# Lightning attention and a leaky-ReLU MLP on one core: the down projection in pairs of groups, partly with seven block products for eight

## The chip, the cores and the metric

The kernel runs on one core of one Trainium2 chip. The metric is device time in microseconds of one execution. TensorE (PE) multiplies; VectorE (DVE), ScalarE (ACT) and GpSimd (POOL) do the elementwise work; SyncE (SP) issues nearly all DMAs, which run on 16 DMA engines.

## What is computed

Inputs are q, k, v of 4 batches, 8 heads, 768 tokens and 64 channels, one decay per head, and two weight matrices. Attention is linear with a decayed state, in blocks of 64 tokens; its result, 3072 tokens by 512, goes through an MLP:

```
x = attn.transpose(0, 2, 1, 3).reshape(3072, 512)
h = x @ w_in                      # 512 -> 2048
g = np.maximum(0.01 * h, h)
out = g @ w_out                   # 2048 -> 512
```

The weights come as float64.

## The kernel before, in words

Tokens are handled in 24 chunks of 128, four chunks to a group (512 tokens), six groups g. The 2048 hidden features are eight slabs p of 256, each of two halves f of 128. Every operand of a large product is split into three parts, a head h, a low part l and a third one m made from both, and each product is three matmuls, h with h, l with l and m with m.

There are two stages. In the *up stage* (with attention interleaved, seen as lines L313, L403 and the att tiles) `up(g, p)` multiplies a slab of w_in with a group: 24 matmuls of 512 columns into one of three rotating banks b (L640), ScalarE scales the bank between the parts (L658) and writes the leaky ReLU into one of two buffers gs (L661), and one DMA stores it to a DRAM tile G (L664). In the same stretch w_out is turned from float64 to float32 (`w_out`, L569 to L585, L617) and then split (`w_out_parts`, L621, L591 to L602) over the w_in slab that is no longer needed.

In the *down stage* each unit, one (g, p), is loaded from G (L675) and split by ScalarE (L682) and VectorE (L683, L685) into one of four ring slots, which lie over the X operands of the up stage. `down(g, p)` has the activations as the stationary operand and w_out as the moving one, so the result lies with tokens in partitions (L700):

```
nc.tensor.matmul(acc[tb][z // 2][:, cols], lhsT=ring[j][z][:, f * T + tb * P:f * T + (tb + 1) * P],
                 rhs=W[pp][z][:, f * d_model:(f + 1) * d_model][:, cols],
```

Four token blocks use the eight banks (psc, po, b and pt). At a group's end ScalarE copies one bank of a token block (L722), VectorE adds the other (L729), and one store of 256 KB in rows of 2 KB goes to the output (L732).

The order on every engine is fixed when the program is built. `Plan.add` takes each operation with an engine, an estimated time, the keys that it reads and writes, and a rank; `Plan.emit` runs through them by earliest start and rank, with one serial DMA queue and lags between engines (3.5 us after a DMA, plus a slack that `move` may set), and emits them in that order. At run time every engine takes its instructions in this order, SP its DMAs too, and each waits for the real events. The list `seq` gives the ranks: rounds of attention, ups, weight steps, then the loads ("dl") and products ("dn") of the down stage.

## Time and profile before

| | us |
|---|---|
| median of 3 runs (lowest, highest) | 611.26 (610.93, 611.92) |
| span of the profiled execution | 609.2 |
| what the median has around that span | 2.1 |
| TensorE busy | 597.9 |
| VectorE busy | 314.0 |
| ScalarE busy | 269.0 |
| up stage, first full TensorE stretch to the first down product | about 47 to 343 |
| down stage | about 343 to 609 |

The profiled execution has its own time only as the span, from its first to its last instruction; the runs' times include what lies around it. A group row of the profile gives line, engine, operation and tiles, then total busy time and the mean of one in ns, then idle time of the engine just before and who ended it. A timeline row gives start and length in us. Matmuls overlap, so their pace is read from a run of them and not from the mean of one.

### The profile page before, as it was taken

The numbers are of one execution on the slowest core, as the hardware profiler recorded it, in microseconds if no ns is written. First come the engines' busy times: TensorE is split into PE (matmuls) and PEld (weight loads), VectorE is DVE, ScalarE is ACT, GpSimd is POOL, SyncE is SP. The second block draws the span as 40 slices with busy tenths as digits, with TensorE's granted clock in tenths as the row PEclk, the third lists the DMA queues.
The fourth block names the chain that finished last, engine by engine and source line by source line (L and its number), as shares of the span: only waits on it lengthen the run. The fifth ranks groups of instructions, "written<-read, shape, count | busy, mean of one in ns | idle before, by whom it ended". The sixth has DMA issues, their size and how long they took to land.

```text
span 609.2 us, 12932 instructions
## 1 busy us (share of the span) xinstructions
PE 597.9 (98%) x5386; PEld 495.6 (81%) x5386; DVE 314.0 (52%) x418; ACT 269.0 (44%) x430; POOL 86.8 (14%) x90
## 2 busy tenths in 40 slices
PE   7899999999999999999999999999999999999997
PEld 6687888888888878888788888888888888888886
DVE  5999764334243426326366745545454544635531
ACT  4688974444455646555577522222222313214111
POOL 1654412104133004104000000000000000000000
PEclk9999999999999999999999999999999999999999
DMA  9998774667888878886686843524333343333201
GB/s 213 232 272 245 221 203 124 173 133 199 199 213 238 212 227 214 216 244 210 233 300 217 290 145 103 173 69 139 138 104 131 112 138 105 138 104 122 86 1 69
DMA packets 147754, 105.18 MB, mean 173 GB/s; under 512 B 123632, under 2 KB 124400, under 8 KB 147696
## 3 DMA queue, kind: packets, MB, share of 16 engines
q1 hardware_dynamic: 147552, 104.36, 58.9%
q8 instruction: 42, 0.69, 0.5%
q14 instruction: 16, 0.13, 0.1%
q10 hardware_dynamic: 144, 0.00, 0.0%
HBM read 68.69 MB, written 35.65 MB: 171 GB/s over the span
## 4 chain that ended last, share of the span: by engine, by line
PE 92%; DVE 4%; DMA 2%; ACT 1%; issue 0%; POOL 0%; SPq 0%; DVEq 0%; ACTq 0%
PE b L640 40%; PE b L700 18%; PE po L700 11%; PE psc L700 11%; PE po L313 4%; PE pt L700 4%; PE psc L313 4%; DMA g<-gs 1%; DMA att<-in_v_dram 1%; DVE w L584 1%; DVE w L585 1%; DVE wm L602 1%; PE pt L403 1%; DMA att<-in_k_dram 1%; DVE wl L596 0%; DVE wh L593 0%
## 5 line engine op out<-in xcount | busy, mean ns | idle before, releaser
L682 ACT ACTIVATE xh<-att 128x1024 fp32r<-128x1024 f32 x48 | 50.7, 1060 | 148.7 <-PE b L700 140.7
L683 DVE SCALAR_TENSOR_TENSOR xl<-att,xh 128x1024 fp32r<-128x1024 f32 x48 | 58.6, 1223 | 98.6 <-ACT xh L682 98.6
L640 PE MATMUL b<-xm,wm 128*128 128x512 f32 (+2 forms) x392 | 104.5, 393 | 0.5 <-ACT b L658 0.5
L640 PE MATMUL b<-xl,wl 128*128 128x512 f32 (+2 forms) x392 | 103.4, 388 | 0.6 <-DVE wl L596 0.6
L640 PE MATMUL b<-xh,wh 128*128 128x512 f32 (+2 forms) x392 | 103.2, 387 | 0.8 <-ACT xh L507 0.8
L640 PEld LDWEIGHTS b<-xh,wh 128*128 128x128 f32 x392 | 73.0, 188 | 15.9 <-ACT xh L507 0.9
L640 PEld LDWEIGHTS b<-xl,wl 128*128 128x128 f32 x392 | 72.8, 188 | 15.6 <-DVE wl L596 1.0
L640 PEld LDWEIGHTS b<-xm,wm 128*128 128x128 f32 x392 | 71.5, 188 | 15.7 <-ACT b L658 0.9
L658 ACT ACTIVATE b<-b 128x512 f32<-128x512 f32 (+2 forms) x97 | 56.1, 580 | 60.3 <-PE b L640 60.1
L661 ACT ACTIVATE gs<-b 128x512 f32<-128x512 f32 (+2 forms) x97 | 56.8, 591 | 44.9 <-PE b L640 38.8
L700 PE MATMUL b<-wl,xl 128*128 128x512 f32 x192 | 74.8, 390 | 0.0
L700 PE MATMUL b<-wh,xh 128*128 128x512 f32 x192 | 74.8, 390 | 0.0
L685 DVE SCALAR_TENSOR_TENSOR xm<-xl,xh 128x1024 fp32r<-128x1024 f32 x48 | 58.7, 1226 | 4.7
L462 POOL TENSOR_TENSOR att<-att 128x256 f32<-128x256 f32 x40 | 35.0, 876 | 57.2 <-DVE att L459 55.9
L700 PEld LDWEIGHTS b<-wl,xl 128*128 128x128 f32 x192 | 36.1, 188 | 7.4
L700 PEld LDWEIGHTS b<-wh,xh 128*128 128x128 f32 x192 | 36.0, 188 | 7.5
L423 POOL TENSOR_TENSOR att<-att 128x512 f32<-128x512 f32 (+1 forms) x20 | 24.2, 1211 | 96.2 <-DVE att L383 47.4
L452 DVE TENSOR_TENSOR att<-psc,att 128x512 f32<-128x512 f32 x24 | 16.5, 690 | 41.0 <-PE psc L313 41.0
L584 DVE TENSOR_SCALAR w<-w 128x512 int32<-128x512 int32 x32 | 19.2, 599 | 35.4 <-ACT w L578 35.3
L700 PE MATMUL po<-wm,xm 128*128 128x512 f32 x96 | 37.4, 390 | 0.0
L700 PE MATMUL po<-wh,xh 128*128 128x512 f32 x96 | 37.4, 390 | 0.0
L700 PE MATMUL po<-wl,xl 128*128 128x512 f32 x96 | 37.4, 390 | 0.0
(73 smaller groups left out, 805.4 us busy)
## 6 DMA issues: line engine op xcount, KB each, us to landing
att<-g SPq DMA_DIRECT2D x48, 512.0 KB, 3.3
g<-gs SPq DMA_DIRECT2D x47, 512.0 KB, 4.0
raw<-in_moe_w_in_dram SPq DMA_DIRECT2D x16, 512.0 KB, 5.4
raw<-in_moe_w_out_dram SPq DMA_DIRECT2D x16, 512.0 KB, 4.7
att<-in_k_dram SPq DMA_DIRECT2D x48, 128.0 KB, 4.2
att<-in_v_dram SPq DMA_DIRECT2D x24, 256.0 KB, 4.4
out_dram<-gs SPq DMA_DIRECT2D x23, 256.0 KB, 2.1
wo<-w SPq DMA_DIRECT2D x8, 512.0 KB, 5.9
```

Of the source, the lines that this page charges most:

```text
L313: nc.tensor.matmul(dst[HALF[cols]], lhsT=lhsT[HALF[rows]], rhs=rhs[HALF[rows]], start=start, stop=True, skip_group_check=True)
L423: add(eng, us, lambda: e.tensor_tensor(o, x, _bc(pow_q, 2, 2)[:, :, m, :], op=ALU.mult), ["fq", dep], [f"qsT{i}"])
L452: add("DVE", 0.69, lambda: nc.vector.tensor_tensor(sc, psc[:, :, lower, :], decay, op=ALU.mult), ["psc", "fk"], ["sc"])
L462: add("POOL", 0.7, lambda new=new, j=j: nc.gpsimd.tensor_tensor(state[(j + 1) % 4], new, _bc(lam_c, 2, D), op=ALU.mult), [f"st{j % 4}", "f ...
L584: add("DVE", 0.42, lambda: nc.vector.tensor_scalar(d, d, 3, None, op0=ALU.logical_shift_left), [], [key])
L640: nc.tensor.matmul(dst, lhsT=w[z][:, kk * 2 * P + f * P:kk * 2 * P + (f + 1) * P], rhs=x[z][:, kk, toks], start=start and kk == 0, stop=kk ...
L658: add("ACT", ns, lambda b=b: nc.scalar.activation(out=b, in_=b, func=AF.Copy, bias=0.0, scale=S + 1.0), [], [kb], rank=-1.5)
L661: add("ACT", ns, lambda b=b, r=r: nc.scalar.activation(out=r, in_=b, func=AF.Prelu, bias=0.0, scale=1.0 / WS, alpha=0.01), [kb], [f"gs{jg} ...
L682: add("ACT", 1.05, lambda: nc.scalar.activation(out=h, in_=graw[j], func=AF.Copy, bias=0.0, scale=NEAR), reads, wr("h"))
L683: add("DVE", 1.25, lambda: nc.vector.scalar_tensor_tensor(l, graw[j], 1.0, h.bitcast(F32), op0=ALU.mult, op1=ALU.subtract), reads + [f"rh{ ...
L685: add("DVE", 1.25, lambda: nc.vector.scalar_tensor_tensor(m, l.bitcast(F32), -S, h.bitcast(F32), op0=ALU.mult, op1=ALU.add), [f"rh{j}", f" ...
L700: nc.tensor.matmul(acc[tb][z // 2][:, cols], lhsT=ring[j][z][:, f * T + tb * P:f * T + (tb + 1) * P], rhs=W[pp][z][:, f * d_model:(f + 1) ...
```

## The change

Groups are handled in three pairs. The operands of the down product change places: w_out is stationary in pieces of 128x128, the activations move 512 tokens at a time, and the result lies with output features in partitions. All three parts of a product now accumulate in one bank, with the scale moved into the up stage's ReLU.

In pair 0, and for slabs p of 4 and more in the other pairs, products are plain: 24 matmuls for a slab and a group (`plain`). For p below 4 in pairs 1 and 2 the products of a slab are taken as 2x2 blocks (two halves f, two halves of the output features, two halves of the tokens of both groups), and seven block products stand for eight (`strassen`), 12 matmuls to a unit of two slabs. Four bank sets X, Y, Z, V take the products; `copy_banks` copies one set to another with ScalarE, `add_banks` adds one set to another through the two halves of gs buffer 0 with ScalarE and VectorE.

The seven products need sums of operands. Those of the activations are made by VectorE in the up stage (`sums`, four operations of 128x256 for each of 16 ups, three of them stored by DMAs of their own, next to the four blocks themselves in one DMA), into a DRAM tile BB of a pair; the other stores to G are split in two by token half. Those of w_out are made in pair 0 (`w_sums`), from the float32 copy in DRAM, over w_out's own second quarter and over memory of attention. The third part of w_out is made in two steps, VectorE and ScalarE (`minus`). The ring has five slots, and a unit is loaded straight into the slot's third part (`unit`). The order of ups in groups 2 to 4 alternates slabs above and below 4, and the slack given to loads of w_out is 0.75 in place of 4.0.

A finished bank leaves by a 32x32 block transpose of VectorE from PSUM into one of two halves of gs buffer 0, and eight stores of 32 partitions each, in pieces of 128 bytes (`leave`).

```diff
     SUBL, FIRST = 0.75, -8.0
 
+    NS = 4
+    LEAD = 8.0
+    WSLACK = 0.75
     DV = 10
...
+    HT = T // 2
+    KINDS_B = ("1", "7", "2", "3", "5", "6", "4")
+    BB = [[dram.tile([P, 7 * 2 * T], F32, name=f"b{r}_{u}", tag=f"b{r}_{u}") for u in range(NS // 2 if r else 0)] for r in range(NG // 2)]
+    G = [{p: dram.tile([P, 4 * T], F32, name=f"g{r}_{p}", tag=f"g{r}_{p}") for p in range(NS if r else 0, NP)} for r in range(NG // 2)]
...
-        move(1.6, get, after, [f"raw{j}"])
+        move(1.6, get, after, [f"raw{j}"], slack=WSLACK)
...
+    def minus(us, x, key):
+        add("DVE", us, lambda: nc.vector.tensor_tensor(x(2), x(1).bitcast(F32), x(0).bitcast(F32), op=ALU.subtract),
+            [key.format("h"), key.format("l")], [key.format("m")])
+        add("ACT", 0.85 * us, lambda: nc.scalar.activation(out=x(2), in_=x(2).bitcast(F32), func=AF.Copy, bias=0.0, scale=1.0 / (S + 1.0)),
+            [], [key.format("m")])
...
+    def w_sums(p):
+
+        j, jr, main, rest = SK[0], SK[1], staging[0], staging[1]
+        b = [main[:, i * NQ:(i + 1) * NQ] for i in range(4)] + [rest[:, i * NQ:(i + 1) * NQ] for i in range(3)]
...
+        def sub(o, x, y, op, reads, k_):
+            add("DVE", 0.42, lambda: nc.vector.tensor_tensor(b[o], b[x], b[y], op=op), reads, k_)
+
+        sub(5, 0, 1, ALU.subtract, j, jr)
+        sub(1, 1, 3, ALU.add, [], j)
+        sub(4, 1, 0, ALU.subtract, j, jr)
+        sub(6, 2, 4, ALU.subtract, j, jr)
+        for key, us, x, src, k_ in ((f"w{{}}{p}", 0.42, lambda z: W[p][z][:, NQ:2 * NQ], b[1], j),
+                                   (f"e{{}}{p}", 0.95, lambda z: more(z, p), rest[:, :3 * NQ], jr)):
+            h, l, m = [key.format(z) for z in "hlm"]
+            add("ACT", 0.9 * us, lambda x=x, src=src: nc.scalar.activation(out=x(0), in_=src, func=AF.Copy, bias=0.0, scale=NEAR / S), k_, [h])
+            add("DVE", us, lambda x=x, src=src: nc.vector.scalar_tensor_tensor(x(1), x(0).bitcast(F32), -S, src, op0=ALU.mult, op1=ALU.add),
+                k_ + [h], [l])
+            if p == NS - 1 and k_ is jr:
+                add("ACT", 0.0, free_lows, [], jr + [m])
+            minus(us, x, key)
...
-        move(1.5 * (hi - lo) / GC + 0.1,
-            lambda: nc.sync.dma_start(out=G[g][p].rearrange("p (f t) -> p f t", f=2)[:, :, toks], in_=y), [f"gs{jg}"], [f"G{g}{p}"], slack=GSLACK)
...
+        if p >= NS or g < 2:
+            d = G[g // 2][p].rearrange("p (f h g t) -> p f h g t", f=2, h=2, g=2)
+            for i in range(2):
+                a, e = max(lo * C, i * HT), min(hi * C, (i + 1) * HT)
+                if a < e:
+                    move(0.75 * (e - a) / HT + 0.1, lambda i=i, a=a, e=e: nc.sync.dma_start(
+                            out=d[:, :, i, g % 2, a - i * HT:e - i * HT], in_=y[:, :, a - lo * C:e - lo * C]),
+                        [f"gs{jg}"], [f"G{g}{p}{i}{lo}"], issue=0.3, slack=GSLACK)
+            return
+        sums(g, p, y.rearrange("p f (h t) -> p f h t", h=2), f"gs{jg}")
...
+    def sums(g, p, y, kg):
+
+        z = spare(g, p)
+        (z0, k0), (z1, k1), (z2, k2) = z
+        (b11, b12), (b21, b22) = [[y[:, f, i, :] for i in range(2)] for f in range(2)]
+
+        def op(o, x, x2, a, reads, writes):
+            add("DVE", 0.42, lambda: nc.vector.tensor_tensor(o, x, x2, op=a), reads, writes, rank=-1.0)
+
+        d = BB[g // 2][p // 2].rearrange("p (k c g t) -> p k c g t", k=7, c=2, g=2)[:, :, p % 2, g % 2, :]
+
+        def store(k, o, key, name):
+            move(0.5, lambda: nc.sync.dma_start(out=d[:, k], in_=o), [key], [f"{name}{g}{p}"], issue=0.15, slack=GSLACK)
+
+        op(z0, b12, b11, ALU.subtract, [kg], [k0])
+        op(b12, b22, b12, ALU.subtract, [], [kg])
+        store(4, z0, k0, "T4")
+        op(z1, b12, b11, ALU.add, [kg], [k1])
+        move(1.6, lambda: nc.sync.dma_start(out=d[:, :4], in_=y.rearrange("p f h t -> p (f h) t")), [kg], [f"B{g}{p}"], slack=GSLACK)
+        store(5, z1, k1, "T5")
+        op(z2, b21, z1, ALU.subtract, [kg, k1], [k2])
+        store(6, z2, k2, "T6")
...
+    acc = {"X": flat[:2], "Z": flat[2:], "Y": [b1[0], b2], "V": [b1[1], bank["pt"]]}
+    ACC = {"X": ["X0", "X1"], "Z": ["Z0", "Z1"], "Y": ["b10", "b2"], "V": ["b11", "pt"]}
...
+    KINDS = {1: (0, "X"), 5: (1, "V"), 6: (-1, "Z"), 2: (2, "X"), 7: (-2, "Z"), 3: (-3, "Y"), 4: (3, "Z")}
+    BANKS = [[("X", 0), ("X", 1), ("Z", 0), ("Z", 1)], [("Y", 0), ("Y", 1), ("V", 0), ("V", 1)]]
...
+        add("DMA", 1.5, go, keys, wr("m"))
+        add("ACT", 1.05, head, [f"rm{j}"], wr("h"))
+        add("DVE", 1.25, low, [f"rm{j}", f"rh{j}"], wr("l"))
+        add("DVE", 1.25, middle, [f"rh{j}", f"rl{j}"], [f"rm{j}"])
+        return j
+
+    def product(dst, j, col, lhs, first=False, n=T):
+        for z in range(3):
+            nc.tensor.matmul(dst, lhsT=lhs(z), rhs=ring[j][z][:, col:col + n], start=first and z == 0, stop=z == 2,
+                             skip_group_check=True)
+
+    def strassen(pr, t, u, lead):
+
+        g = 2 * pr
+        ps_ = (2 * u, 2 * u + 1)
...
+        w, d = KINDS[t]
+
+        def go():
+            for i, p in enumerate(ps_):
+                for c in range(2):
+                    product(acc[d][c], j, i * T, lambda z, p=p, c=c: operand(z, p, w)[:, c * P:(c + 1) * P],
+                            first=t in (1, 5) and u == 0 and i == 0)
+        add("PE", 0.227 * 12, go, [f"r{z}{j}" for z in "hlm"] + [f"{'w' if w >= 0 else 'e'}{z}{p}" for z in "hlm" for p in ps_],
+            ACC[d])
...
+    def plain(pr, p, gi, lead, last=False, banks=None):
...
+        def go(fs, cs, lo=0, n=T):
+            for f in fs:
+                for c in cs:
+                    d, i = BANKS[gi][c]
+                    product(acc[d][i][:, lo:lo + n], j, f * T + lo,
+                            lambda z, f=f, c=c: W[p][z][:, f * 2 * NQ + c * P:f * 2 * NQ + (c + 1) * P], first=pr == p == f == 0, n=n)
+
+        if not last:
+            add("PE", 0.227 * 24, lambda: go((0, 1), range(4)), reads, [ACC[d][i] for d, i in BANKS[gi]])
+            return
+        for c in banks:
+            d, i = BANKS[gi][c]
+            very_last = pr == NG // 2 - 1 and gi == 1 and c == banks[-1]
+            for half in range(2 if very_last else 1):
+                k = ACC[d][i] + (f"half{half}" if very_last else "")
+                n = T // (2 if very_last else 1)
+                add("PE", 0.227 * 6 * (0.53 if very_last else 1.0), lambda c=c, half=half, n=n: go((0, 1), (c,), half * n, n),
+                    reads + ([ACC[d][i]] if very_last else []), [k])
+                leave(pr, gi, c, acc[d][i], ACC[d][i], k, half * n, n)
+
+    def leave(pr, gi, c, b, kb, k, lo, n):
+        nonlocal n_o
+        o, n_o = n_o % 2, n_o + 1
+        y = gs[0][:, o, lo:lo + n]
+        add("DVE", 0.1 + 0.6 * n / T, lambda: nc.vector.transpose(out=y, in_=b[:, lo:lo + n]), [kb, k], [f"o{o}"] + (["gs0"] if n_o <= 2 else []), rank=-1.5)
+
+        def store():
+            for a in range(4):
+                for m in range(lo // HT, (lo + n) // HT):
+                    t0 = (2 * pr + m) * T + gi * HT
+                    nc.sync.dma_start(out=out[t0:t0 + HT, c * P + a * C4:c * P + (a + 1) * C4].rearrange("(b i) j -> i b j", i=C4),
+                                      in_=y[a * C4:(a + 1) * C4, m * HT - lo:(m + 1) * HT - lo].rearrange("i (b j) -> i b j", j=C4))
+
+        add("DMA", 1.7 * n / T, store, [f"o{o}"], [], rank=-1.5)
+
+    def copy_banks(d, s):
+        for i in range(2):
+            add("ACT", 0.6, lambda i=i: nc.scalar.copy(acc[d][i], acc[s][i]), [ACC[s][i]], [ACC[d][i]], rank=-1.5)
+
+    def add_banks(d, s):
+        for i in range(2):
+            y, key = gs[0][:, i, :], [f"o{i}"] + (["gs0"] if n_o == 0 else [])
+            add("ACT", 0.6, lambda i=i, y=y: nc.scalar.copy(y, acc[s][i]), [ACC[s][i]], key, rank=-1.5)
+            add("DVE", 0.72, lambda i=i, y=y: nc.vector.tensor_tensor(acc[d][i], acc[d][i], y, op=ALU.add), [f"o{i}"], [ACC[d][i]], rank=-1.5)
...
+    ORDER = [4, 0, 5, 1, 6, 2, 7, 3]
+    steps = [(g, p) for g in range(2, NG) for p in (ORDER if g < NG - 1 else range(NP))]
...
-    for g in range(NG):
-        for p in range(0, NP, 2):
-            seq += [("dl", g, p), ("dl", g, p + 1), ("dn", g, p)]
+            if p == NS - 1:
+                seq.append(("fr",))
+    for pr in range(NG // 2):
+        def s(t, u):
+            return "s", pr, t, u
+
+        def n(p, gi, r=pr):
+            return ("n", r, p, gi) if p < NP - 1 else ("l", r, p, gi, (0, 1, 2, 3) if gi == 0 else (2, 3, 0, 1))
+
+        late = [n(p, 1, pr - 1) for p in range(NS, NP)] if pr else []
+        if pr:
+            seq += [late[0], s(1, 0), late[1], s(1, 1), ("copy", "Z", "X"), late[2], s(6, 0), late[3], s(6, 1), ("copy", "Y", "Z"),
+                    s(5, 0), s(5, 1), ("add", "Y", "V"), s(7, 0), s(7, 1), ("add", "V", "Z"),
+                    s(3, 0), n(4, 0), s(2, 0), n(5, 0), s(3, 1), s(2, 1), n(6, 0), s(4, 0), s(4, 1), n(7, 0)]
+        else:
+            i = seq.index(("up", NG - 1, NP - 1))
+            seq[i:i] = [n(0, 0)]
+            seq += [n(0, 1), n(1, 0), n(1, 1), ("ws", 0), n(2, 0), n(2, 1), ("ws", 1), n(3, 0), n(3, 1), ("ws", 2), n(4, 0), n(5, 0), ("ws", 3), n(6, 0), n(7, 0)]
+    seq += [n(p, 1) for p in range(NS, NP)]
```

## The prediction

> **What bounds the kernel now.** I read the page's busy shares first, then the chain that ended last, then windows, and then the groups, DMA issues and timeline of the places that the change touches.
>
> ```profile
> span 609.2 us, 12932 instructions
> PE 597.9 (98%) x5386; PEld 495.6 (81%) x5386; DVE 314.0 (52%) x418; ACT 269.0 (44%) x430; POOL 86.8 (14%) x90
> PE 92%; DVE 4%; DMA 2%; ACT 1%; issue 0%; POOL 0%; SPq 0%; DVEq 0%; ACTq 0%
> ```
>
> TensorE is busy for 98% of the span and carries 92% of the chain; the rest of the chain lies in the first 47 us, which the change hardly touches. So a matmul taken out is worth its full pace, as long as nothing else then comes late. The windows show how much room the others have:
>
> ```profile
> 180.00:345.00 165.00, 164.24 (x1679) 135.58 (x1678) 77.76 (x118) 98.58 (x169) 25.52 (x28) 1.00 0.80 236
> 215.00:260.00 45.00, 44.52 (x536) 36.53 (x535) 18.12 (x32) 25.61 (x46) 10.30 (x12) 1.00 0.84 225
> 300.00:345.00 45.00, 45.00 (x201) 37.25 (x200) 27.96 (x29) 30.75 (x49) 0.00 (x0) 1.00 0.78 268
> 432.00:605.00 173.00, 173.00 (x767) 143.42 (x766) 81.45 (x76) 39.30 (x46) 0.00 (x0) 1.00 0.30 103
> ```
>
> After the length come PE, PEld, DVE, ACT and POOL, the granted clock, the DMA share and GB/s. In the up stage (180 to 345) the DMA engines are 80% busy and VectorE 47%. In the down stage (432 to 605) TensorE has no idle time, the clock is 1.00, VectorE is at 47% and the DMA engines at 30%. The stage's grain, from the chain in order of time, the groups, the DMA issues and the timeline:
>
> ```profile
> 368.93 2.72 PE po L700 x12
> L683 DVE SCALAR_TENSOR_TENSOR xl<-att,xh 128x1024 fp32r<-128x1024 f32 x48 | 58.6, 1223 | 98.6 <-ACT xh L682 98.6
> L459 DVE TENSOR_TENSOR att<-att,psc 128x256 f32<-128x256 f32 x40 | 16.4, 410 | 1.1 <-POOL att L462 1.0
> L383 DVE STREAM_TRANSPOSE att<-raw 128x512 f32<-128x512 f32 x2 | 1.3, 688 | 0.0
> g<-gs SPq DMA_DIRECT2D x47, 512.0 KB, 4.0
> 95.73 3.80 SPq L374 DMA_DIRECT2D raw<-in_k_dram  x7
> 604.50 1.11 PE L700 MATMUL pt<-wm,xm 128*128 128x256 f32 x8
> 605.71 0.76 DVE L729 SCALAR_TENSOR_TENSOR gs<-pt,raw 128x256 f32<-128x256 f32 x2 [1.72 <-PE pt L700]
> L732 SPq DMA_DIRECT2D out_dram<-gs x25: 332/338/383, 382.1 to 606.6; - x25
> ```
>
> Twelve matmuls take 2.72 us, 0.2267 each. The last matmul ends at 605.6, the last store's issue starts at 606.6 and the span ends at 609.2: a tail of 3.6 us, 2.6 of them after that issue. Each of the 25 output stores costs SP 0.34 us.
>
> **The change part by part.** *Matmuls.* Pairs 1 and 2 replace, for p below 4, 192 matmuls by 7 x 2 x 12 = 168 of the same shape: 48 fewer in all, -10.9 us, all on the path. The last bank, in halves, takes 12 x 0.139 = 1.66 in place of 1.36, where before 8 halves took 1.11 in place of 0.91: +0.1.
>
> *Unit preparation.* There are 60 units in place of 48, each with one load, one ACT copy (1.06) and two VectorE operations (1.22): 12 x 2.45 = +29 us of VectorE. A seven-product unit feeds 2.72 us of TensorE and needs 2.45 us of VectorE, so in a row of six of them VectorE stands at 90%. The cover is the ring of five units. Over a pair VectorE has 22 x 2.45 + 8 transposes and 4 bank adds of 0.69 = 62 us against 81.6 of TensorE. I cost this at nothing by itself; it makes every late unit slow to catch up.
>
> *Weight sums* (four in pair 0): 1.7 us of small subtractions and 2.7 of splitting on VectorE, 2.4 on ACT each. With 16 units VectorE has 57 of pair 0's 87 us; hidden by that. The two-step third part adds 8 x 1.06 of ACT in the last group of the up stage, 30.75 + 8.5 of 45 us there; hidden. Zero-cost markers moved from VectorE to POOL issue nothing.
>
> *Sums of activations* (16 ups): 64 operations of 128x256 at 0.41 (the L459 row) are 26 us of VectorE, in 165 us with 87 idle. Three stores of 128 KB more for each, 6.3 MB; at the window's 225 GB/s for a share of 0.84 that is 24 us of DMA, share 0.80 to about 0.94. In most of the other 33 ups one store becomes two, +0.35 us of SP each. The buffer gs is the narrow place: an up is 24 x 0.2267 = 5.44 us, so from the last ScalarE write of one up to the first write two ups later there are about 7.5 us. Before, a landing of 4.0 fits. Now two VectorE operations (0.82) and one more issue (0.4) come ahead of the large store, and the DMA engines are fuller: 5.3 us without queueing. The large store's wait stands in SP's queue ahead of later k, q and v loads; a late landing holds ScalarE's Prelu and with it the scaling of the next bank, which TensorE waits for. In before ScalarE waited twice on such a landing (2.4 us in the waits), and TensorE's idle time in 215 to 260 is 0.5 us. Weight loads are now planned with 0.75 us of slack where they land in 4.7, which can hold ScalarE likewise. Ends: 0 (all fits) and +8 (half a microsecond in each of the 16). More than the 0.8 us of idle TensorE in 180 to 345 can't be gained. I take +2, four such events of the size seen.
>
> *Output, the main term.* A 512-token bank now leaves as transposed 32x32 blocks: the transpose costs 0.69 like the operation that it replaces, but one store of 0.34 becomes eight on the same SP queue, of 32 KB each in 128-byte pieces. No such store is in the trace. The nearest row is the transposed load of the same 32 KB: seven in 3.80 us, 0.54 with the slow second one of a run, 0.5 otherwise. The far row is the plain store, 0.34 + 0.05 between issues. I take 0.5, since the shape is the same and only the direction differs: 4.0 to 4.4 us of SP for each leave, 16.8 for four in a row, where banks are ready every 1.36 us.
>
> The tail, from the end of the first of the last four banks: first leave transposed by 0.75, its stores issued 0.8 to 5.1; second 5.1 to 9.1; third 9.1 to 13.1; first half 13.1 to 15.1; the second half shares its buffer with the third leave and waits for that to land (12.6 + 2.0) and for its transpose: stores 15.1 to 17.1, the last starting at 16.6. The end is 2.6 later, 19.2. TensorE ends at 2.72 + 1.66 = 4.4. Tail 14.8 in place of 3.6: +11.2. With 0.39 an issue it is 11.7: +8.1.
>
> The same queue inside: when a pair's second group leaves at the start of the next pair, TensorE goes on with six seven-product units. Counted again from the first bank's end: the copies of Z to Y need the fourth leave's transpose (10.7 to 11.4, after its buffer's earlier stores landed) and finish at 12.0, just before the 12.2 at which Z is written again. But adding V to Y borrows the two output buffers: the second comes free when the fourth leave's last store has landed, 17.1 - 0.5 + 2.0 = 18.6, then 0.6 of ScalarE and 0.7 of VectorE: 20.0. Product 3 into Y is due at 4.1 + 5 x 2.72 = 17.7. TensorE waits 2.3 us, about 3 with the two unit loads that stand between those stores on SP. ScalarE, waiting in order for that buffer, holds the splitting of later units, and SP their loads. Ends: 0 (0.39 an issue gives 16.2, ahead of 17.7) and 6.5 (product 3's load stands behind all stores: issued at 17.1, landed 3.3 later, 1.06 and 2.45 of splitting, 24). I take 3, twice: +6. The first group's leaves are followed by 16 us of prepared units and cost nothing.
>
> The Trainium skill, "DMA: Bandwidth & Descriptors", section Specifications, speaks against these stores: under 512 B a transfer is said to be a read-modify-write. In this sum the 128-byte pieces matter only above 0.5 x 16 / 256 = 31 ns a piece, since SP is slower up to there; by that rule, with a piece at twice the loads' time (at most 16 ns: in the timeline, nine issues of 384 pieces in 6 us, in which the DMA share was 0.58 of 16 engines), the sum would not change.
>
> Sum: -10.9 + 0.1 + 2 + 11.2 + 6 = +8.4, span 617.6. The profiled span of 609.2 lies 2.1 below the median of 611.26 with what is around it; so 619.7, said as 620.
>
> **Rivals.** *The issue is cheap* (other side): at the plain store's 0.39 the tail is +8.1 and product 3 does not wait: -10.9 + 0.1 + 8.1 + 0 to 2 = -2.7 to -0.7; at 0.34 with nothing between, +6.8 and so -4 to -2. Say 609. For it: direction SBUF to DRAM has only 0.34 rows. Against: these have few pieces and one dimension. With nothing lost elsewhere the tail alone cancels the gain at some 0.49 us an issue; with the up stage's +2, at 0.42.
>
> *The tail is paid, the middle is not:* other units fill ScalarE and VectorE, Y is ready in time: -10.9 + 0.1 + 11.2 + 0 to 2, 611.7 to 613.7, say 612.5. For it: five units in the ring. Against: the borrowed buffer is a true dependence.
>
> *The up stage becomes bound by its stores:* landings past 7.5 us in half of the sums: +8 in place of +2, 626. For it: DMA share 0.94. Against: 40% idle VectorE, and stores spread over every second up.
>
> *The pieces are slow:* writes of 128 bytes at 50 ns hold SP to 0.8 us an issue; the tail is +20 and each inner wait 11: about 645. For it only that no write so small has run; against it, the loads' 16 ns at most. The skill's rule named above points this way.
>
> **How the numbers follow.** Forecast 0.50 (its own range 614 to 625), cheap issue 0.17, tail alone 0.15, up stage 0.13, slow pieces 0.05. A measurement can tell about 0.2% (1.2 us) from no change: faster takes the cheap issue and a little of the tail-alone case, 0.19; same 0.07, from these two; slower 0.74. The range 607.5 to 630 leaves out the slow pieces and the ends of the others.
>
> **What would show it.** The down stage has 1,104 matmuls in place of 1,152 (six and four of them as halves), still 12 in 2.72 us. SP: runs of eight output issues at 0.5. After the last matmul about 15 us with only SP, DMA and two transposes. Inside each of pairs 1 and 2, TensorE idle some 3 us ahead of a product into b (Y), released by VectorE's add. In the up stage ScalarE's Prelu waiting for DMA from gs. Wrong would be: issues at 0.4 or below, no idle TensorE in the pairs, or a tail under 11 us.

## The result and the profile after

The changed kernel takes 654.23 us (median; 652.51 to 656.9) beside 611.59 for the kernel before: a ratio of 1.0699, interval 1.0671 to 1.0727. The forecast was 620, its range 607.5 to 630: the sign is right, the size is not. The profiled execution has a span of 653.3 us and a time of 655.04.

The page after, span, busy shares, granted clock in 40 slices, and the chain's shares:

```profile
span 653.3 us, 13542 instructions
PE 603.9 (92%) x5340; PEld 492.1 (75%) x5340; DVE 386.1 (59%) x544; ACT 293.7 (45%) x460; POOL 86.3 (13%) x90
PEclk9999999999989899898999999999999999989996
PE 44%; DMA 7%; SPq 7%; DVE 4%; issue 2%; ACT 2%; DVEq 0%; ACTq 0%
```

TensorE has fallen from 98% to 92% of the span and from 92% to 44% of the chain. What took its place is not VectorE (59%) but DMA and SPq, SP's queue, which had 0% of the chain before. The windows (length; busy us and instructions of PE, PEld, DVE, ACT, POOL; granted clock, DMA share, GB/s) show three kinds of place:

```profile
160.00:180.00 20.00, 15.46 (x185) 12.15 (x184) 7.32 (x15) 8.77 (x16) 2.31 (x3) 0.95 0.86 221
460.00:500.00 40.00, 33.58 (x139) 25.49 (x138) 27.82 (x27) 12.70 (x15) 0.00 (x0) 1.00 0.53 148
560.00:600.00 40.00, 34.58 (x138) 26.16 (x137) 25.82 (x26) 13.85 (x16) 0.00 (x0) 0.96 0.54 157
640.00:653.00 13.00, 0.00 (x0) 0.00 (x0) 1.62 (x3) 0.00 (x0) 0.00 (x0) 0.58 0.36 61
```

The up stage (first line) has idle TensorE where before it had 0.8 us in 165. At the start of pairs 1 and 2 (second and third line) there are 139 and 138 matmuls, at 0.2267 31.5 and 31.3 of 40 us: 8.5 and 8.7 are lost (the busy time counts some of it, since ends are modelled). Before, nothing was lost in the whole down stage. At the end only SP, DMA and two transposes are left.

The loss can be divided into four terms. "Up stage" is the end of the last up matmul (from its start in the line's own view, plus 0.227) less the down matmuls already done by then at 0.2267 each: 344.3 us before, 370.0 after. "Tail" is the span's rest after the last matmul. "Down stage" is what lies between, less its matmul records at 0.2267: 1156 records before, 1110 after (a record or two can be missing).

| us | before | after | difference | predicted |
|---|---|---|---|---|
| matmuls of the down stage | 262.1 | 251.6 | -10.4 | -10.8 |
| up stage | 344.3 | 370.0 | +25.7 | +2 |
| down stage beyond its matmuls | -0.7 | 16.9 | +17.6 | +6 |
| tail | 3.6 | 14.7 | +11.1 | +11.2 |
| sum (span; terms rounded) | 609.2 | 653.3 | +44.0 | +8.4 |

*The tail* came out as worked out. The store's own view (count, ns lowest/median/highest, first and last start), then SP's and VectorE's timeline at the end:

```profile
L882 SPq DMA_DIRECT2D out_dram<-gs x192: 315/449/1618, 433.5 to 650.6; - x192
DMA to landing us min/median/max: 1.5/1.7/4.7
```

```profile
614.75 18.27 SPq L882 DMA_DIRECT2D out_dram<-gs  x32
...
635.15 15.94 SPq L882 DMA_DIRECT2D out_dram<-gs  x32
...
640.43 0.72 DVE L876 STREAM_TRANSPOSE gs<-b 128x512 f32<-128x512 f32 x1 [3.94 <-DMA out_dram<-gs]
...
648.57 0.45 DVE L876 STREAM_TRANSPOSE gs<-b 128x256 f32<-128x256 f32 x1 [3.89 <-DMA out_dram<-gs]
```

The first group's 32 stores are out at 633.0, and SP waits 2.1 us for the first transposed bank of the second group. From there on it is the queue of 32 that the prediction counted: 15.94 / 32 = 0.50 us apiece, the last issue at 650.6 and the end 2.6 us later. VectorE waits 3.9 us for a buffer whose earlier stores must land before each late transpose. The pieces of 128 bytes land after 1.7 us at the median, as quickly as any store here: the price is SP's issue, not the pieces.

*The pairs.* SP's, VectorE's, ScalarE's and TensorE's timeline at the head of pair 1 (each row: start, length, engine, what, and the idle time before it with its releaser):

```profile
472.35 0.87 SPq L796 DMA_DIRECT2D xm<-b  x2
473.31 8.73 SPq L882 DMA_DIRECT2D out_dram<-gs  x16
...
471.35 0.57 ACT L889 COPY b<-po 128x512 f32<-128x512 f32 x1 [6.52 <-DVE gs L876]
476.54 1.06 ACT L800 ACTIVATE xh<-xm 128x1024 fp32r<-128x1024 f32 x1 [1.68 <-DMA xm<-b]
483.46 0.59 ACT L894 COPY gs<-pt 128x512 f32<-128x512 f32 x1 [3.33 <-DMA out_dram<-gs]
486.91 1.06 ACT L800 ACTIVATE xh<-xm 128x1024 fp32r<-128x1024 f32 x1 [2.86 <-DMA xm<-g]
...
474.91 3.03 PE L818 MATMUL po<-raws,att 128*128 128x512 f32 x12 [1.39 <-ACT b L889]
488.02 0.50 PE L818 MATMUL psc<-xh,wh 128*128 128x512 f32 x1 [0.84 <-ACT xh L800]
```

Sixteen stores hold SP from 473.3 to 482.0. ScalarE, which works in order, waits 6.5 us to copy Z to Y (for the transpose that waits for landed stores), splits two units, waits 3.3 us for the add's borrowed buffer, and only then comes to the next units. The units' loads stand behind the stores as well (L796 in the first row; the next goes out at 482.1). TensorE loses a little at each: Z not yet copied, the first parts of a unit late, Y's add, the next unit.

*The up stage* has six idle stretches of TensorE of more than 1.5 us after 160 us (4.4, 1.6, 2.0, 1.8, 2.3 and 2.1, together 14.2). The first of them on SP, ScalarE and TensorE, and the waits of the whole span (total us, times, longest):

```profile
171.96 1.19 SPq L733 DMA_DIRECT2D g<-gs  x2
173.25 0.56 SPq L577 DMA_DIRECT2D raws<-in_moe_w_out_dram  x1
...
177.64 0.66 ACT L586 ACTIVATE w<-raws 128x512 f32<-128x512 f32 x1 [5.74 <-DMA raws<-in_moe_w_out_dram]
...
180.12 3.78 PE L702 MATMUL b<-xm,wm 128*128 128x512 f32 x8 [4.37 <-ACT b L720]
```

```profile
PE b L702 <- ACT b L720: 7.0, 3, 4.4
PE b L702 <- ACT gs L725: 5.1, 3, 2.1
ACT w L586 <- DMA raws<-in_moe_w_out_dram: 15.4, 5, 5.7
ACT lows L588 <- DMA raws<-in_moe_w_out_dram: 11.5, 5, 4.1
```

All six begin alike. ScalarE, in its fixed order, stands for 3.0 to 5.7 us on a load of w_out (L586 or L588), does the conversions, and only then what TensorE needs of it (scaling, ReLU, a split or a step of attention). Each of the six loads was issued within 0.1 us of the end of the DMA ahead of it on SP, so it was SP's queue that held it; it landed 4.4 to 5.8 us after its issue. In the kernel before, ScalarE does not wait for a load of w_out at all between 165 and 345 us. The buffer gs, which the prediction called the narrow place, holds the ReLU on a landing store only once here, for 1.2 us. Which part of the change makes these loads late, the experiments had to say.

### The profile page after: what moved, and what is told of

It reads as the page before. It is cut to its first block, busy times and chain, and to the rows that moved or that the text cites. A ratio compares the mean times of both kernels' runs of the same rounds, so it can differ in the third digit from the quotient of the medians.

```text
span 653.3 us, 13542 instructions
## 1 busy us (share of the span) xinstructions
PE 603.9 (92%) x5340; PEld 492.1 (75%) x5340; DVE 386.1 (59%) x544; ACT 293.7 (45%) x460; POOL 86.3 (13%) x90
## 4 chain that ended last, share of the span: by engine, by line
PE 44%; DMA 7%; SPq 7%; DVE 4%; issue 2%; ACT 2%; DVEq 0%; ACTq 0%
PE b L702 14%; PE psc L818 9%; PE po L818 9%; PE b L818 7%; SPq L882 5%; DMA xm<-b 2%; PE pt L818 2%; DMA raws<-in_moe_w_out_dram 2%; DVE xl L804 1%; DMA xm<-g 1%; PE po L320 1%; SPq L381 1%; DMA att<-in_k_dram 1%; PE psc L320 1%; DVE gs L876 1%
## 5 line engine op out<-in xcount | busy, mean ns | idle before, releaser
L702 PE MATMUL b<-xh,wh 128*128 128x512 f32 (+2 forms) x392 | 106.5, 397 | 7.7 <-ACT gs L725 5.1
L800 ACT ACTIVATE xh<-xm 128x1024 fp32r<-128x1024 f32 x48 | 50.9, 1060 | 94.9 <-DMA xm<-g 54.9
L702 PEld LDWEIGHTS b<-xm,wm 128*128 128x128 f32 x392 | 73.8, 195 | 23.9 <-ACT b L720 8.4
L804 DVE SCALAR_TENSOR_TENSOR xl<-xm,xh 128x1024 fp32r<-128x1024 f32 x48 | 58.5, 1219 | 44.5 <-ACT xh L800 40.9
L430 POOL TENSOR_TENSOR att<-att 128x512 f32<-128x512 f32 (+1 forms) x20 | 24.6, 1232 | 111.5 <-DVE att L390 56.6
L320 PEld LDWEIGHTS po<-att 64*64 64x64 f32 x1472 | 28.1, 139 | 11.2 <-issue 6.0
L320 PE MATMUL po<-att 64*64 64x64 f32 x1472 | 33.8, 227 | 2.3 <-ACT att L498 1.6
L592 DVE TENSOR_SCALAR w<-w 128x512 int32<-128x512 int32 x32 | 16.9, 528 | 29.7 <-ACT w L586 29.5
L426 POOL TENSOR_TENSOR att<-att 128x512 f32<-128x512 f32 (+1 forms) x23 | 26.4, 1149 | 56.6 <-DMA att<-in_k_dram 20.1
L818 PE MATMUL b<-xl,wl 128*128 128x512 f32 (+1 forms) x86 | 33.0, 384 | 0.0
L818 PE MATMUL b<-xm,wm 128*128 128x512 f32 (+1 forms) x86 | 33.0, 384 | 0.0
L818 PE MATMUL b<-xh,wh 128*128 128x512 f32 (+1 forms) x86 | 33.0, 384 | 0.0
L588 ACT ACTIVATE lows<-raws 128x512 uint16<-128x512 uint32 x32 | 25.0, 781 | 13.4 <-DMA raws<-in_moe_w_out_dram 11.5
```

What stands on the lines that cost most here:

```text
L320: nc.tensor.matmul(dst[HALF[cols]], lhsT=lhsT[HALF[rows]], rhs=rhs[HALF[rows]], start=start, stop=True, skip_group_check=True)
L426: lambda e="POOL": ENG[e].tensor_tensor(kr[nr], kr[nr], _bc(pow_k, 3, D)[nr], op=ALU.mult), ["fk"], [f"k{i}"])
L588: add("ACT", 0.78, lambda: nc.scalar.activation(out=addend(U16, 0), in_=words(0, U32), func=AF.Copy, bias=0.0, scale=2.0 ** -29), [f"raw{j ...
L702: nc.tensor.matmul(dst, lhsT=w[z][:, kk * 2 * P + f * P:kk * 2 * P + (f + 1) * P], rhs=x[z][:, kk, toks], start=start and kk == 0, stop=kk ...
L800: nc.scalar.activation(out=h, in_=m.bitcast(F32), func=AF.Copy, bias=0.0, scale=NEAR)
L804: nc.vector.scalar_tensor_tensor(l, m.bitcast(F32), 1.0, h.bitcast(F32), op0=ALU.mult, op1=ALU.subtract)
```

## The experiments

Theories after the result. A: SP's issue time is what the up stage ran out of; the added stores hold the loads and the stores that free gs. B: the weight loads' slack of 0.75 lets ScalarE stand on them. C: the sums of activations (VectorE, the DMA bytes) are the cost. For the pairs: D, SP's runs of output stores; E, the two buffers shared by leaves and adds; F, the seven-product rows, in which VectorE stands at 90%.

**One part at a time, taken from the changed kernel.** e_rows lets a bank leave by one store:

```diff
-            for a in range(4):
-                for m in range(lo // HT, (lo + n) // HT):
...
+            r0 = ((2 * pr + gi) * 4 + c) * P
+            nc.sync.dma_start(out=out[r0:r0 + P, lo:lo + n], in_=y)
```

> The changed kernel, but a finished bank leaves by one store of 128 rows of 2 KB in place of eight stores of 32 KB; the transposed blocks land in other places of the output, so the output's order is left out. If the eight stores on SP's queue are what makes the tail (14.8 us after the last matmul begins to end, 3.6 before) and the two holes of TensorE inside the pairs (8 us each by its gaps), both go: 11 + 16 us, 654 to about 627, with the up stage unchanged. If the holes come from VectorE at 90% in the rows of seven-product units, only the tail goes: about 643.

e_slack gives the weight loads their slack of 4.0 back; e_noT leaves out the three separate stores of sums, so the result lacks the products of the sums; e_all3 does all three.

```diff
-        move(1.6, get, after, [f"raw{j}"], slack=WSLACK)
+        move(1.6, get, after, [f"raw{j}"])
...
-            move(0.5, lambda: nc.sync.dma_start(out=d[:, k], in_=o), [key], [f"{name}{g}{p}"], issue=0.15, slack=GSLACK)
+            return
```

> The changed kernel with the old slack of 4.0 us in place of 0.75 for the loads of w_out, and nothing else. The up stage is some 26 us longer than before. If ScalarE is held in order by conversions that were planned ahead of their loads, most of the up stage's holes (4.5, 2.1, 1.9, 2.5, 2.3 us and what the slower clock adds after them) go: 15 to 25 us, 630 to 640. If the queue of SP is what makes those loads late, and any plan meets that, less than 5 us: 650 to 654.

> The changed kernel without the 48 stores of the sums of activations (the sums are still made by VectorE); three of the seven kinds of units are loaded from the plain blocks instead, so the products of the sums are left out of the result, and the amount of work on TensorE is the same. If the stores' places in SP's queue and their DMA time make the up stage late, it gains 12 to 25 us: 630 to 642. If the planned slack does, or VectorE's sums, under 6 us: 648 to 654.

> The three edits together: one store of rows per bank, the old slack, no stores of sums (order of the output and products of the sums left out). If these three are the whole of the loss, what is left is the 48 matmuls fewer, with the sums' VectorE work hidden: 611.6 - 10.8 + 0 to 3, 601 to 604. If VectorE's sums in the up stage or its 90% in the pairs cost by themselves, 606 to 615.

| | span | up stage | down beyond matmuls | tail | ratio |
|---|---|---|---|---|---|
| e_rows | 622.0 | 366.9 | -1.2 | 4.7 | 1.0209 (1.0163 to 1.0255) |
| e_slack | 650.1 | 362.7 | 21.2 | 14.6 | 1.0629 (1.0551 to 1.0707) |
| e_noT | 649.9 | 364.1 | 19.5 | 14.6 | 1.0631 (1.0561 to 1.07) |
| e_all3 | 609.6 | 353.7 | -0.7 | 5.0 | 0.9976 (0.9951 to 1.0001) |

e_rows bears D out: with one store where there were eight, tail and pair holes go together, 29.8 us between the medians (654.23 to 624.44), with the same units, copies, adds and two buffers. Each of the two single repairs of the up stage gives 6 to 7 us there, and some of it is lost again later. And even with all three costs away, the kernel with fewer products only equals the one before: 9.4 us of the up stage are still missing.

**The tail and the buffers.** g_tail takes the last four units bank by bank, so that a bank is finished every 5.4 us; g_adds gives leaves four buffers and adds one of their own; g_plan tells the planner the measured prices of the stores and has the slack of 4.0.

```diff
+        for c in banks:
+            for p, j in units:
...
-        o, n_o = n_o % 2, n_o + 1
-        y = gs[0][:, o, lo:lo + n]
+        o, n_o = n_o % 4, n_o + 1
+        y = gs[o // 2][:, o % 2, lo:lo + n]
...
-        add("DMA", 1.7 * n / T, store, [f"o{o}"], [], rank=-1.5)
+        add("DMA", 4.4 * n / T, store, [f"o{o}"], [], rank=-1.5)
```

> The changed kernel with the last four units taken bank by bank: a bank is ready every 5.44 us in place of 1.36, so that its eight stores (4.3 us of SP) are issued before the next. If the tail is SP's queue of stores, it falls from 14.8 to about 5 us (half a transpose, four stores at 0.5, 2.6 after the last issue), -9.8: 654.2 to about 644.5. If the transposed stores are slow to land, less than 5 us are won.

> The changed kernel with four output buffers in place of two (both halves of both gs) and with the adds of V to Y and Z to V through w32 in place of the output buffers. If the borrowed and scarce buffers make the holes inside the pairs, both go: -16, 638. If it is unit loads that stand behind the stores in SP's queue, 5 us of each 8 stay: 644 to 650. The tail changes by less than 1.5 us, since SP is the limit there.

> The changed kernel with the measured prices in the list that orders the queues: eight output stores 4.4 us in place of 1.7, the stores of blocks and sums 0.5 in place of 0.15 and 0.3, the slack 4.0. Nothing else changes but the order. If the order was planned by too low prices, the loads come ahead of the stores in time: the holes in the up stage and the pairs shrink by half or more, 654 to 630 or less; the tail stays. If SP is full whatever the order, it gives what the slack alone gave: 646 to 651.

None helps, and g_adds and g_plan lie above both ranges that were expected of them: spans 656.0, 654.7 and 661.9, ratios 1.0746 (1.0677 to 1.0814), 1.073 (1.067 to 1.079) and 1.0851 (1.0796 to 1.0906). SP's timeline in g_tail says why this order of banks hardly shortens the tail (12.8):

```profile
619.48 34.41 SPq L914 DMA_DIRECT2D out_dram<-gs  x64
```

Bank by bank, the second group's first bank is finished at 626.9, but the first group's stores of the same pair hold SP until 637.8. Here the tail is a queue of 64, and the expectation had counted only the last four banks. In g_adds the copies no longer wait for buffers, and the down stage still loses 23.4, so E alone is not the cause. g_plan, with another order on every queue, loses 30.2 there, against 21.2 for e_slack, which has the same slack.

**Fewer issues, another queue.** h_even makes the halves of the tokens from even and odd blocks of 32, so four stores of 64 KB serve for eight; h_pool sends the eight from GpSimd's queue.

```diff
-                    nc.sync.dma_start(out=out[t0:t0 + HT, ...
+                    nc.gpsimd.dma_start(out=out[t0:t0 + HT, ...
```

> The changed kernel with the token halves taken as even and odd blocks of 32 tokens (ScalarE writes them apart), so that the blocks of both groups merge into one step and a bank leaves by four stores of 64 KB in place of eight of 32 KB, the same bytes in the same 128-byte pieces. If the number of issues on SP is what costs, the tail falls by about 6 us (14.8 to 8.7) and most of the 16 us of holes in the pairs go: 654 to 632 to 640. If the pieces themselves are slow, an issue takes twice as long and nothing is won: 650 to 655.

> The changed kernel with the eight stores of a bank issued from POOL's queue, which is empty in the down stage, in place of SP's. If the holes in the pairs come from unit loads behind the stores in SP's queue, they shrink from 16 us to under 6; if from the borrowed output buffers, they stay or grow. The tail depends on POOL's price for an issue, which no run has shown: with 0.5 us it stays at 15, with 1 us it is about 30 and the buffers come free later. 638 to 675.

The edit shown is h_pool's. h_even: span 634.1, down stage 2.1 in place of 16.9, tail 9.3 in place of 14.7; ratio 1.0334 (1.0195 to 1.0473). Half the issues, with the same bytes in the same pieces, remove most of the holes, so it is the number of issues and not the pieces: D. h_pool: 657.6, ratio 1.0775 (1.0724 to 1.0827), with a tail of 19.5, because GpSimd takes longer for each. The store's view:

```profile
L882 POOL DMA_DIRECT2D out_dram<-gs x192: 582/582/745, 431.6 to 653.4; - x192
```

In h_pool no load stands behind a store, and the down stage still loses 19.3: TensorE now waits for the adds and copies that need the output buffers (14.2 us in all). In g_adds the buffers are free, and it waits for units and for copies behind them. So each of the two paths is enough to make the holes, and taking away one of them leaves the other; they go when the runs of eight stores go (e_rows, h_even).

**Without seven products.** g_plain takes plain products everywhere (so no sums, no copies, no adds), with the rest of the change; h_up also has the slack of 4.0 and one store per up, loaded in two pieces.

```diff
-    NS = 4
+    NS = 0
...
-                    move(0.75 * (e - a) / HT + 0.1, lambda i=i, a=a, e=e: nc.sync.dma_start(
...
+            d = G[g // 2][p].rearrange("p (g f t) -> p g f t", g=2, f=2)[:, g % 2, :, toks]
+            move(1.5 * (hi - lo) / GC + 0.1, lambda: nc.sync.dma_start(out=d, in_=y),
```

> The changed kernel's layout and stores without the seven products: every slab in every pair is a plain product (48 matmuls back in), no sums are made or stored, each up stores its two token halves; the slack of 0.75 stays. The tail stays at +11. If the holes inside the pairs come from the output stores meeting the short seven-product units and the borrowed buffers, they go, as 5.44 us units lie behind the stores. If the up stage's loss comes from the sums and their stores, it goes too: 611.6 + 11 + 0 to 4 = 623 to 627. If it comes from the slack and the doubled stores, it stays: 640 to 650.

> The all-plain kernel in the new layout (649.5 us) with the old slack of 4.0 and one store of rows of 4 KB for an up in place of two in pieces of 1 KB; a plain unit is loaded in two pieces instead. Its up stage lost some 18 us, the one before 2. If the slack and SP's longer queue of stores are the up stage's loss, it falls to 2 to 5: 649.5 - 13 to -16 = 633 to 637. If something else in the up stage costs (w_out's single buffer of low words, the third part in two steps, the order of the ups), 640 or more.

g_plain: 647.3, up stage 360.1, down 10.2, ratio 1.0629 (1.0579 to 1.068). h_up: 638.6, up stage 346.3, down 15.0, ratio 1.0483 (1.0416 to 1.055). So 15.8 of the 25.7 us of the up stage come without any sum of activations, which C can't explain, and 13.8 of these go when the two small repairs are made. The two repairs were not taken apart here. In the down stage F falls: plain units have the holes too, at the same place, and e_rows has the seven-product rows and no holes. TensorE's waits in h_up:

```profile
PE b L819 <- DVE gs L877: 9.1, 2, 5.0
```

**Two parts alone, in the kernel before.** d_before splits its one store per up in two token halves; s_before sets only the slack of 0.75.

```diff
-        move(1.5 * (hi - lo) / GC + 0.1,
-            lambda: nc.sync.dma_start(out=G[g][p].rearrange("p (f t) -> p f t", f=2)[:, :, toks], in_=y), ...
+        for i in range(2):
+            a, e = max(lo * C, i * 256), min(hi * C, (i + 1) * 256)
+            if a < e:
+                move(0.75 * (e - a) / 256 + 0.1, lambda a=a, e=e: nc.sync.dma_start(
+                        out=G[g][p].rearrange("p (f t) -> p f t", f=2)[:, :, a:e], ...), [f"gs{jg}"], [f"G{g}{p}"], issue=0.3, slack=GSLACK)
```

> The kernel before with the store of an up split in two, one for each token half. If one issue more for an up (49 in all, 0.35 to 0.6 us each on SP) is enough to make the loads late, it loses 4 to 10 us: 615 to 621. If SP still has room, under 2: 611 to 613.

> The kernel before with a planned slack of 0.75 us in place of 4.0 for the loads of w_out. If ScalarE's conversions, planned ahead of their loads, hold the up stage by themselves, it loses 5 to 14 us: 617 to 626. If the slack only hurts where SP's queue is long, under 3: 610 to 614.

s_before: 617.21, ratio 1.0114 (1.0079 to 1.0148): B is real, 5.5 us. d_before: 635.38, ratio 1.0387 (1.0354 to 1.042), up stage 368.8, the down stage and the tail unchanged, far beyond the 615 to 621 that were expected. The store's view in d_before, then a stretch of the chain in order of time (start, length, what):

```profile
L666 SPq DMA_DIRECT2D g<-gs x97: 513/519/1727, 38.5 to 378.6; - x97
```

```profile
213.09 0.52 SPq L666
...
219.97 4.14 DMA g<-gs
...
224.22 0.60 ACT gs L661
...
224.87 5.49 PE b L640 x12
```

ScalarE's ReLU had filled this gs at 208.1. Its first half goes out at 213.1 and its second, behind six loads of k and q (L374), one of w_out (L569) and one store of its float32 form (L617), at 220.0. It lands after 4.1 us; ScalarE's next ReLU waits for the buffer, and TensorE for ScalarE. Each half also costs more to issue than the whole: 519 ns against 351 for L664 before.

The 23.7 us of d_before are not the price of one issue more, though. In its plan both halves write the same key, so the plan takes the second for one that must follow the first's landing (a lag of 3.5 us and a slack of 2.0) and puts other DMAs between them. In the changed kernel and in g_plain each half has a key of its own, and the halves go out next to each other, 0.6 us apart. d_before shows that a store which leaves late can fill the up stage by itself; the size for the change has to come from g_plain and h_up, 13.8 us together with the slack. With the 4.7 that s_before's up stage loses from the slack, some 9 would be left for the second stores, an estimate that holds only if the two add up.

**Both repairs, and the whole put together.** u_fix is the changed kernel with slack 4.0 and one store per plain up. b2 adds to that h_even's blocks, sums merged into two stores or one, four buffers, the tail bank by bank and half of the last stores from ScalarE's queue; q_nosum is b2 without VectorE's sums and their stores, so without the products of the sums in the result; b3 is b2 with output stores from GpSimd (the last group's shared over three queues) and 2 us of slack for the reload of w_out; p_plain is b3 with plain products only.

```diff
+            add("ACT", 0.5, lambda: store((0,), nc.scalar), [f"o{o}"], [], rank=-1.5)
+            add("POOL", 0.6, lambda: store((1,), nc.gpsimd), [f"o{o}"], [], rank=-1.5)
+            add("DMA", 1.0, lambda: store((2, 3), nc.sync), [f"o{o}"], [], rank=-1.5)
```

> The changed kernel with the old slack of 4.0 and one store of rows of 4 KB for an up without sums, everything else as it is. In the all-plain kernel these two took the up stage's loss away. If they are its cause here too, 15 to 20 of its 24 us go: 654 to 634 to 640. If the sums' own stores and operations keep it, it stays near what the slack alone gave: 645 to 651.

> The seven products with all repairs: slack 4.0; one store of rows for an up; two or one store for the three sums; even and odd blocks, so four stores for a bank; four output buffers and adds through w32; the last four units bank by bank, their stores half from ScalarE's queue. If SP's queue and the slack are the whole loss, what stays is 48 matmuls fewer, up stage 2 to 5 us longer, no holes in the pairs, a tail of 5 in place of 3.6: 611.5 - 10.8 + 2 to 5 + 1.5 = 604 to 607. If VectorE's extra work costs by itself, 608 to 616.

> The repaired kernel (619.6 us) without VectorE's sums of activations and their stores; the units of sums are loaded from plain blocks, so the products of the sums are left out of the result, with the same work on TensorE. If the sums make what is left of the up stage's holes (9 us of TensorE's time from 160 to 345), it gains 6 to 9: 611 to 614. If they hide, less than 2: 618 to 620.

> The repaired kernel (619.6 us) with the four output stores of a bank issued from POOL's queue, at 0.58 each as the run from POOL showed, except in the last group, where they are shared by three queues; and with 2 us of planned slack for the reload of w_out. If unit loads behind output stores are what is left of the pairs' holes (5.5 us) and the late reload what is left of the up stage's (5.8 us), it gains 6 to 11: 609 to 614. If those holes are VectorE's 90%, they stay: 616 to 620.

> The same kernel as the one beside it, with all plain products in place of the seven: 48 matmuls more (+10.8 us of TensorE), no sums, 12 units fewer. If the repairs leave nothing but a tail of 5 to 6 us in place of 3.6, it is at 612 to 615, and the seven products are worth what their own waits leave of 10.8. If the new layout costs by itself, over 617.

| | span | up stage | down beyond matmuls | tail | median, ratio |
|---|---|---|---|---|---|
| u_fix | 649.8 | 366.0 | 17.6 | 14.6 | 651.35, 1.0644 (1.0608 to 1.0681) |
| b2 | 616.4 | 353.5 | 5.2 | 6.1 | 619.63, 1.0124 (1.0051 to 1.0197) |
| q_nosum | 611.2 | 346.3 | 7.1 | 6.2 | 615.04, 1.0059 (1.0024 to 1.0095) |
| b3 | 627.7 | 359.0 | 12.2 | 4.9 | 626.56, 1.0252 (1.0229 to 1.0274) |
| p_plain | 613.1 | 345.8 | 0.1 | 4.7 | 615.75, 1.0081 (1.0063 to 1.0099) |

b2 and b3 lie above both ranges that were expected of them (up to 616 and up to 620), and u_fix at the upper end of the worse of its two. Two repairs that restored the up stage without sums (h_up) hardly help with them (u_fix), and moving the stores to GpSimd's queue made b3 slower than b2, not faster. One figure goes with the up stage's loss through all these kernels, the time that SP spends on issuing the stage's stores, added up over its queue until the last up is done (21.0 us before):

| kernel | SP on these stores beyond before | up stage beyond before |
|---|---|---|
| p_plain, q_nosum, h_up | -0.4, -0.3, 0.0 | 1.5, 2.0, 2.0 |
| s_before (slack alone) | 0.4 | 4.7 |
| b2, b3 | 14.2, 14.7 | 9.2, 14.7 |
| e_noT, e_all3, u_fix | 23.9, 24.5, 27.7 | 19.8, 9.4, 21.7 |
| g_plain, d_before | 35.9, 38.6 | 15.8, 24.5 |
| e_slack, e_rows, after | 52.2, 52.5, 53.3 | 18.4, 22.6, 25.7 |

No kernel without added issue time loses over 2.0 us unless its slack is cut, and none with 14 us or more loses under 9. (The five kernels that are not in the table have 53 to 58 and lose 21 to 27.) So the added issues are needed for the loss, but they don't give its size: e_all3 and u_fix, with 24.5 and 27.7 and the same slack, lose 9.4 and 21.7, and g_plain and d_before, with much the same issue time, 15.8 and 24.5. Every one of these edits also gives the plan another order on all engines, and what the order does was not separated. ScalarE's waits for loads of w_out follow the queue and the slack: 26.9 us after the change, 18.4 in g_plain, 12.3 in s_before and at most 3.6 in p_plain, q_nosum and h_up. With the slack back and SP as busy as after the change (e_slack) they are still 16, and the ReLU's waits for DMAs rise from 1.6 to 11. SP's queue is busy for 79% of 165 to 285 us after the change and 90% or so in 195 to 225 and 255 to 285; before, 66%, with two stretches of 15 us at 0.92 among it.

The sums with their merged stores still cost 7.2 us (b2 against q_nosum, up stage; 4.6 between the medians). No run separates VectorE's operations from those stores, so C is not excluded for this part. And the seven products come out behind plain ones in like kernels: b3 lies 10.8 us above p_plain (median against median) although its matmuls save 10.9, and b2, with more of the stores on SP, still 3.9 above it. No kernel here beats the one before: p_plain is 0.8% slower, 1.1 us of it the tail and 1.5 the up stage; e_all3 only matches it.

*Open:* b3's down stage still loses 12.2 and b2's and q_nosum's 5 to 7. In b3 TensorE's waits name the adds into Y:

```profile
PE b L824 <- DVE b L937: 8.1, 2, 4.1
```

What makes these adds late, the units' splitting ahead of them or SP's loads, was not separated.

## Why the prediction was right or wrong

- **Matmuls, -10.8 predicted:** -10.4 by the records.
- **Tail, +11.2:** measured +11.1. The price of 0.5 us an issue, taken from the transposed load of the same shape, was right (0.49 from one issue to the next at the median), as were the wait for the first transposed bank and the end after the last issue. So "cheap issue" fell, and "slow pieces" too: the rule of the Trainium skill, "DMA: Bandwidth & Descriptors", section Specifications, under which transfers below 512 B are read-modify-writes, shows no cost here, the 128-byte stores landing in 1.7 us at the median.
- **Waits inside the pairs, +6:** measured +17.6. The mechanism was right in its parts (stores ahead of loads on SP, leaves that wait for buffers, ScalarE in order), and h_even and e_rows show that the runs of stores make them; 3 us each should have been some 8.5, beyond the upper bound of 6.5. I had followed one chain, to the add into Y, and let the later of its waits count; in the trace the waits come one after another on ScalarE (copy, unit, add, unit), and TensorE loses at four places; at the add itself, where I put all of it, 1.1 us. "I cost this at nothing by itself", said of the 12 added units, was not the failing part: plain units lose as much (h_up).
- **Up stage, +2, the step that failed (measured +25.7):** two things that the prediction named had no price in the sum. One is SP: "In most of the other 33 ups one store becomes two, +0.35 us of SP each", and four DMAs for each of the 16 ups with sums. SP's load was never measured, since the windows have no column for SP. It was busy for 66% of 165 to 285 us before. The 65 halves then took 38.9 us of it and the 64 DMAs of the ups with sums 37.2, where 49 stores had taken 21.0. The other is the weight loads: "planned with 0.75 us of slack where they land in 4.7, which can hold ScalarE likewise". The trace after shows the two together: all six holes begin with ScalarE standing on a load of w_out that SP had issued without a pause behind other DMAs. The prediction looked for the wait at gs instead, where it cost 1.2 us. g_plain against h_up gives 13.8 us to the cut slack and the second stores of the ups. The sums and their stores go with most of the rest (after against g_plain, 9.9), and how that splits between SP and VectorE stays open. The rival "bound by its stores" came nearest, with another reason (landings past 7.5 us, DMA share 0.94) and so with the wrong size, +8. In the window 160 to 180 the DMA share is 0.86, hardly above the 0.80 to 0.84 of before.
- **A reading of the profile before** that hid this: the rest of the chain does not lie in the first 47 us alone. From 213.2 to 223.7 us the chain before leaves TensorE for SP, a store of gs that lands after 5.46 us, and ScalarE's conversions of w_out. The stage had hardly any room there even before the change.
- **The slack alone** costs 5.5 us in the kernel before (s_before), where SP is busy for 66% of 165 to 285 us. It was named as a risk and had no term of its own.
- **VectorE** is not the limit, as predicted: e_rows, with the same work for it, loses nothing in the down stage (-1.2).
- **The clock** was taken as 1.00 throughout. It isn't once TensorE stops; the last section has the sizes.

The likeliest case had 0.50 and its two wrong terms lay outside the bounds that I had given them (up to +8 for the up stage, up to 13 for the pairs), so the range could not hold the time.

## What to carry to other kernels

Count the issues on each queue as one counts the instructions of an engine: add up SP's time in the stage concerned before adding a DMA to a step that repeats, and look at what stands behind it in the same queue. Here the second stores of the ups and a cut slack cost 13.8 us (g_plain against h_up), while the DMA engines were hardly fuller (a share of 0.83 against 0.80 in 165 to 285 us). Look also at whose order is fixed: one late load on an engine that works in order holds everything behind it, and a bound from one chain of such waits is no upper bound. A saving in TensorE's work has to be set against the issues that its operands need: here 10.9 us of matmuls came with 53 us more of SP's time in the up stage, and p_plain, which takes the plain products, beats its twin b3. And when a kernel's order comes from a plan, an edit "of one thing" can change the order too: compare the order of the queues before reading its price (d_before).

## What the runs showed of the hardware

*The clock after short holes.* Windows of the changed kernel, two holes and what follows them, then a stretch chopped into shorter ones (columns as above, the clock third from the end):

```profile
175.50:180.00 4.50, 0.25 (x2) 0.00 (x0) 1.64 (x5) 2.36 (x4) 0.00 (x0) 0.77 1.04 276
180.00:184.00 4.00, 3.88 (x14) 2.65 (x17) 2.41 (x4) 1.64 (x5) 1.28 (x1) 0.50 0.75 275
...
223.00:226.00 3.00, 1.04 (x5) 0.52 (x4) 1.35 (x3) 2.90 (x6) 0.00 (x0) 0.96 0.55 90
226.00:229.00 3.00, 3.00 (x9) 2.35 (x8) 1.38 (x4) 0.45 (x1) 0.00 (x0) 0.50 0.94 245
...
487.00:490.00 3.00, 1.18 (x3) 0.37 (x2) 1.90 (x2) 2.96 (x5) 0.00 (x0) 1.00 1.03 391
```

After a hole of 4.4 us the granted clock is 0.50 from 178.0 to 184.8, 6.83 us; after one of 2.0 to 2.1 us (223.4 or 223.6 to 225.5, by the matmuls' pace or their modelled ends) it is 0.50 for 3.41 us. Between 487 and 490 TensorE is idle for 1.8 us of 3, but never for more than some 1.0 at a time, and keeps 1.00. A stretch of 3.41 at half speed costs up to 1.7 us on top of the hole. The up stage has five such places, 20.5 us in all and in part inside the holes, so at most some 10 of its 25.7 us lie here; the kernel before had a clock of 1.00 from 180 to 345. The Trainium skill, "TensorE: Matmul & The Clock Gate", section "Why this matters for your kernels", warns of gaps over about 3 us; here 2.1 were enough. They were not always: s_before has a hole of 2.26 us (175.75 to 178.01) and keeps 1.00 after it.

*Issue times.* A plain store of rows costs SP 338 ns (the 25 of e_rows), a store in 1 KB pieces 519 (d_before), one in 128-byte pieces 449 from SP and 582 from GpSimd.
